# First x tile loaded in two column halves, and x, keys and values on one load queue in order of need: one change to the start of an attention kernel

## The chip, the cores and the metric

The kernel runs on one core of a Trainium2 chip. The metric is the device time of one execution in microseconds (us). A profile also gives a span, from the first to the last instruction; here the device time is about 1.8 us above it.

## The reference

`x` is 2048 x 512. It is normalised, goes through 32 heads of attention against cached keys and values (2048 x 128 per head), and through a two-layer network whose output gates the result.

```python
xn = layernorm(x)
q = (xn @ wq) per head                      # 32 heads of 128
p = softmax(q @ k.T * 128 ** -0.5)          # k, v: 32 x 2048 x 128
s = (p @ v) @ wo
g = silu(relu(xn @ w1 + b1) ** 2 @ w2 + b2)
out = x + s * g
```

## The kernel before

The program is a list of instructions for each engine, issued in order. What matters here is the start. The loads are issued from two queues, SP (SyncE) and AC (ScalarE):

```python
    ln_load(0, 0, SP)          # x tile 0, 128 rows
    ln_load(0, 1, AC)          # x tile 1
    load_k0(0)                 # keys of head 0, first half (SP)
    fill_wq(0, AC)             # query weights of head 0
    load_k0(1)                 # keys of head 0, second half (SP)
    E(AC, partial(_act, out=th_t[:, 0, 0:1], in_=warm[:, 0:1], func=ACT.Exp), deps=[t_warm])
    ln_load(0, 2, SP)
    ln_load(0, 3, SP)
    fill_wq(1)
    load_v0(0)
    load_v0(1)
    # ... further loads on SP
```

The work begins with 36 matmuls on zeros, which only keep TensorE busy. Then come the keys, transposed on TensorE, and the first x tile:

```python
    warm_up(36)
    k0_transpose(0)            # TensorE, 8 transposes, waits for the first half of the keys
    k0_copy(0)
    ln_bn(0, 0)                # VectorE, statistics of x tile 0
    ln_rstd(0, 0, eng=DV)
    ln_bn(0, 1)                # statistics of x tile 1
    ln_scale(0, 0)
    first_transpose(0)         # TensorE, 4 transposes of the scaled tile
    k0_transpose(1)            # TensorE, waits for the second half of the keys
    k0_copy(1)
    # ...
    first_copy(0)
    first_proj(0)              # TensorE, waits for the query weights
```

TensorE takes these in exactly this order, so the first half of the keys holds up everything behind it. About 1230 us of dense work follow.

The softmax here doesn't subtract the row's maximum and nothing guards it: scores larger than these inputs give would overflow.

## Time and profile before

| | before |
|---|---|
| device time, first three runs | 1237.87 us median (1237.75 to 1238.44) |
| span of the profiled run | 1236.3 us |
| TensorE busy | 1231.7 us (100%) |
| first half of the keys: issued, landed | 1.18, 5.20 us |
| last warm-up matmul ends | 5.00 us |
| first matmul on head 0's values | 9.68 us |

The prediction below shows the lines that carry this and reads them: the chain of the first 16 us, the timeline beside it, and the time of each load from issue to landing. The last row of the table is the start of the first eight matmuls named `psO<-v_sb,pT` in the timeline.

### The profile page before, as it was taken

What the parts mean: (1) busy time and instruction counts of PE and PEld (TensorE: products, weight loads), DVE (VectorE), ACT (ScalarE), POOL (GpSimd) and SP (SyncE); (2) the same over time, 40 slices, a digit from 0 to 9 for tenths busy, and PEclk for the clock granted to TensorE, in tenths of its full rate; (3) what the DMA queues carried; (4) which work ended last, traced back from release to release, by engine and by line L of the source; (5) the groups of instructions that cost most, each with busy time, mean ns of one, the idle gap of its engine ahead of it and who ended that gap; (6) DMA issues with size and microseconds to landing.
All of it is one profiled execution on the core that took longest, in us unless ns stands there. A gap on an engine that the chain in (4) does not pass through costs nothing.

```text
span 1236.3 us, 26934 instructions
## 1 busy us (share of the span) xinstructions
PE 1231.7 (100%) x11885; PEld 818.8 (66%) x11885; DVE 472.8 (38%) x953; ACT 1053.5 (85%) x1044; POOL 31.9 (3%) x73
## 2 busy tenths in 40 slices
PE   9999999999999999999999999999999999999999
PEld 7666666666666666666666666666666666666665
DVE  4453323244435332334444532333344333324333
ACT  7888888888888888888888888888888888888885
POOL 1010000000002000000000200000000000000000
PEclk9999999999999999999999999999999999999999
DMA  9999998777879897778778878787788789878771
GB/s 211 203 231 209 185 178 134 130 144 143 139 152 172 141 161 129 139 139 145 133 133 170 172 138 143 141 148 134 133 146 148 146 154 158 137 134 146 145 123 31
DMA packets 686868, 185.41 MB, mean 150 GB/s; under 512 B 673536, under 2 KB 685568, under 8 KB 686752
## 3 DMA queue, kind: packets, MB, share of 16 engines
q1 hardware_dynamic: 684656, 179.62, 80.4%
q0 software_dynamic: 1424, 3.81, 1.2%
q8 instruction: 94, 1.54, 0.6%
q10 hardware_dynamic: 672, 0.26, 0.1%
q14 instruction: 22, 0.18, 0.1%
HBM read 96.60 MB, written 2.10 MB: 80 GB/s over the span
## 4 chain that ended last, share of the span: by engine, by line
PE 99%; DMA 0%; DVE 0%; issue 0%; SPq 0%; DVEq 0%
PE psO L157 38%; PE psA L152 36%; PE psF L152 25%; DMA kT<-in_A_k_cache_dram 0%; PE psA L157 0%; DVE out_t L165 0%; PE psF L196 0%; DVE tmp_t L175 0%; PE psO L196 0%; PE psO L152 0%; DVE xnT L179 0%; SPq L208 0%; PE psA L196 0%; DVEq L119 0%
## 5 line engine op out<-in xcount | busy, mean ns | idle before, releaser
L161 ACT ACTIVATE pT<-psA 128x1024 bf16<-128x1024 f32 x1024 | 1043.5, 1023 | 163.5 <-PE psA L152 118.1
L157 PEld LDWEIGHTS psO<-v_sb,pT 128*128 128x128 bf16 x8192 | 547.7, 98 | 240.5 <-issue 12.5
L157 PE MATMUL psO<-v_sb,pT 128*128 128x129 bf16 x8192 | 631.6, 220 | 0.0
L152 PE MATMUL psA<-qt_sb,kT 128*128 128x512 bf16 x2032 | 604.8, 379 | 0.0
L179 DVE COPY o_un<-psO 128x258 f32<-128x258 f32 x256 | 97.4, 422 | 399.4 <-PE psO L157 398.7
L152 PE MATMUL psF<-xnT,wq_sb 128*128 128x512 bf16 (+1 forms) x520 | 168.9, 374 | 0.2 <-DVE xnT L179 0.2
L152 PE MATMUL psF<-wo_all,oT 128*128 128x512 bf16 x480 | 163.8, 379 | 0.0
L152 PEld LDWEIGHTS psA<-qt_sb,kT 128*128 128x128 bf16 x2032 | 156.9, 98 | 0.0
L179 DVE CAST qt_sb<-psF 128x512 bf16<-128x512 f32 (+1 forms) x130 | 88.0, 677 | 97.4 <-PE psF L152 97.4
L165 DVE TENSOR_TENSOR o_bf<-o_un,rden 128x512 bf16<-128x512 f32 x128 | 88.6, 692 | 4.7 <-DVE rden L183 0.3
L152 PEld LDWEIGHTS psF<-xnT,wq_sb 128*128 128x128 bf16 x520 | 50.2, 98 | 60.1 <-issue 0.3
L171 DVE TENSOR_SCALAR r_t<-psF,b1f 128x512 bf16<-128x512 f32 x56 | 42.0, 750 | 117.5 <-PE psF L152 117.5
L152 PEld LDWEIGHTS psF<-wo_all,oT 128*128 128x128 bf16 x480 | 46.9, 98 | 56.4
L152 PE MATMUL psF<-xnT,w_sb 128*128 128x512 bf16 x224 | 77.1, 379 | 0.0
L152 PE MATMUL psF<-w_sb,h2T 128*128 128x512 bf16 x224 | 74.2, 379 | 0.0
L152 PEld LDWEIGHTS psF<-xnT,w_sb 128*128 128x128 bf16 x224 | 21.9, 98 | 26.5
L152 PEld LDWEIGHTS psF<-w_sb,h2T 128*128 128x128 bf16 x224 | 21.9, 98 | 26.5
L165 DVE TENSOR_TENSOR z_t<-psF,b2bc 128x512 f32<-128x512 f32 x16 | 11.1, 692 | 67.2 <-PE psF L152 67.2
L165 DVE TENSOR_TENSOR acc<-psF,acc 128x512 f32<-128x512 f32 x28 | 19.3, 689 | 29.9 <-PE psF L152 29.9
L208 POOL DMA_DIRECT2D out_dram<-out_t x12 | 6.7, 554 | 891.0 <-DVE out_t L165 891.0
L165 DVE TENSOR_TENSOR h2T<-r_t 128x512 bf16<-128x512 bf16 x56 | 23.8, 425 | 1.9
L183 DVE RECIPROCAL rden<-o_un 128x4 f32<-128x4 f32 x128 | 22.9, 179 | 4.4
(47 smaller groups left out, 165.6 us busy)
## 6 DMA issues: line engine op xcount, KB each, us to landing
v_sb<-in_A_v_cache_dram SPq DMA_DIRECT2D x127, 512.0 KB, 4.7
wq_sb<-in_A_wq_dram SPq DMA_DIRECT2D x127, 128.0 KB, 3.1
wo_all<-in_A_wo_dram SPq DMA_DIRECT2D x4, 1024.0 KB, 6.7
w_sb<-in_B_w_dram SPq DMA_DIRECT2D x14, 256.0 KB, 4.3
oT<-o_bf SPq DMA_TRANSPOSE x128, 4.0
x_t<-in_A_x_dram POOLq DMA_DIRECT2D x16, 128.0 KB, 3.4
kT<-in_A_k_cache_dram SPq DMA_TRANSPOSE x127, 4.5
x_ln<-in_A_x_dram SPq DMA_DIRECT2D x15, 128.0 KB, 3.8
```

What stands on the lines that cost most here:

```text
L152: return e.matmul(out, lhsT, rhs, start=start, stop=stop)
L157: return e.matmul(out, lhsT, rhs, start=start, stop=stop, skip_group_check=True)
L161: return e.activation(out, in_, func, bias=bias, scale=scale)
L165: return e.tensor_tensor(out, in0, in1, op)
L171: return e.tensor_scalar(out, in0, scalar1=scalar1, scalar2=scalar2, op0=op0, op1=op1)
L179: return e.tensor_copy(out, in_)
L183: return e.reciprocal(out, in_)
L208: return e.dma_start(out, in_)
```

## The change

The intent: x tile 0 should be ready sooner, by reducing its left half while the right half still lands; and one queue, SP, should carry x, the keys and the values in the order in which they are needed, so that nothing less urgent is moved beside them. The first query weights stay on ScalarE's queue, where the first Exp, with its table load, now stands ahead of them.

```diff
-    ln_load(0, 0, SP)
-    ln_load(0, 1, AC)
+    HD = D // 2
+    sl_x0 = S.slot("x0b")
+    t_x0 = [S.emit_dma(SP, partial(_dma, out=x_ln[:, 0, c:c + HD], in_=A_x[0, 0:P, c:c + HD]), sl)
+            for c, sl in ((0, sl_xl[0]), (HD, sl_x0))]
+    ln_load(0, 1, SP)
     load_k0(0)
-    fill_wq(0, AC)
     load_k0(1)
     E(AC, partial(_act, out=th_t[:, 0, 0:1], in_=warm[:, 0:1], func=ACT.Exp), deps=[t_warm])
+    fill_wq(0, AC)
...
-    ln_bn(0, 0)
-    ln_rstd(0, 0, eng=DV)
+    for b in range(2):
+        t_xl[0] = t_x0[b]
+        ln_bn(0, 0, b * HD, (b + 1) * HD)
+    ln_rstd(0, 0, n=2, eng=DV)
     ln_bn(0, 1)
```

More of the change, by code (lines that the diff above doesn't have):

```diff
@@ L898, in bass_recurrent_scan__mha_block_cached__dense_activation_squared_relu__prompt_kernel @@
         at(j * SPB + SPB // 2, partial(load_xt, j))
-    HD = D // 2
     warm_up(36)
```

## The prediction

> **What bounds the kernel now.** I read the page first: busy shares, then the chain that ended last. Then I went to the first 16 us alone, because the diff only touches instructions emitted there.
>
> ```profile
> span 1236.3 us, 26934 instructions
> PE 1231.7 (100%) x11885; PEld 818.8 (66%) x11885; DVE 472.8 (38%) x953; ACT 1053.5 (85%) x1044; POOL 31.9 (3%) x73
> ...
> PE 99%; DMA 0%; DVE 0%; issue 0%; SPq 0%; DVEq 0%
> ```
>
> TensorE is busy 1231.7 of 1236.3 us and is 99% of the chain. It idles only 4.6 us: about 1 us before its first instruction, a few tenths around 5 to 8 us, and the rest in the output tail after 1231.5 us. So a change at the start can pay in one way only: TensorE's real work begins earlier or later and the whole 1230 us behind it shifts by that amount. The chain of the first 16 us says what that start hangs on (columns: start us, us, what):
>
> ```profile
> 0.73 0.40 SPq L208
> 1.12 0.06 issue
> 1.18 4.02 DMA kT<-in_A_k_cache_dram
> 5.20 0.05 issue
> 5.24 0.94 PE psO L196 x8
> 6.19 0.24 PE psF L196 x4
> 6.43 0.02 issue
> 6.45 0.43 DVE xnT L179
> 6.89 0.14 issue
> 7.02 0.38 PE psF L152 x4
> ```
>
> The gate is not the x tile but the first half of head 0's keys. SP issues it second, at 1.18; it lands at 5.20, and eight transposes of it come first in TensorE's order. Only after them come the four transposes of the normalised x tile, its copy, and the first projection, which needs the first query weights. The timeline of the same stretch shows what sits beside that chain:
>
> ```profile
> 0.72 0.40 ACTq L208 DMA_DIRECT2D x_ln<-in_A_x_dram  x1
> 0.73 0.40 SPq L208 DMA_DIRECT2D x_ln<-in_A_x_dram  x1
> ...
> 0.98 4.02 PE L152 MATMUL psA<-warm 128*128 128x128 bf16 x36 [0.98 <-POOL mhalf L187]
> ...
> 1.15 0.45 ACTq L208 DMA_DIRECT2D wq_sb<-in_A_wq_dram  x1
> 1.18 1.00 SPq L208 DMA_DIRECT2D kT<-in_A_k_cache_dram  x2
> ...
> 1.63 1.28 ACT L161 ACT_TABLE_LOAD   x1 [1.63 <-PEq L1025]
> ...
> 3.71 0.69 DVE L200 BATCH_NORM_STATS2 st_t<-x_ln 128x6 f32<-128x512 bf16 x1 [3.71 <-DMA x_ln<-in_A_x_dram]
> ...
> 5.50 0.41 DVE L171 TENSOR_SCALAR xn_t<-x_ln,mv_t,rstd 128x512 bf16<-128x512 bf16 x1
> ```
>
> Two things are to be seen. The warm-up matmuls fill TensorE from 0.98 to 5.00, so the key transposes could not start before 5.00 even if the keys were there: only 0.24 us of real waiting stands before 5.24. And the x path has slack: the scaled tile is ready at 5.91, while its transposes run only after the key transposes end, at 6.18. The DMA view cut down to these issues gives issue to landing (last column, us):
>
> ```profile
> kT<-in_A_k_cache_dram SPq DMA_DIRECT2D x1, 256.0 KB, 4.0
> x_ln<-in_A_x_dram ACTq DMA_DIRECT2D x1, 128.0 KB, 2.7
> x_ln<-in_A_x_dram SPq DMA_DIRECT2D x1, 128.0 KB, 3.0
> wq_sb<-in_A_wq_dram ACTq DMA_DIRECT2D x1, 128.0 KB, 4.2
> ```
>
> The first x tile lands at 3.7, the second at 3.4, the keys' first half at 5.2, the query weights at 1.15 + 4.2 = 5.35. In stretches of 0.2 us the DMA share is under 0.4 until 2.4 us and then stays near 1.0 at about 310 GB/s: from there the engines are shared, and what is queued beside a load decides when it lands.
>
> **What the Trainium skill says.** "DMA: Bandwidth & Descriptors", section "Issuing engines are not separate DMA queues": DMAs from different engines run on the same 16 DMA engines; issuing from two saves only issue time. The trace agrees: SP and ACT issue side by side at 0.73 and 0.72, 0.40 us each, then the share sits at 1.0. So moving x tile 1 to SP costs SP one issue and wins no bandwidth by itself. The same page, "Rules for kernel authors", says that transfers under 64 KB pay mostly overhead; the halves are exactly 64 KB. The trace shows the issue side of it: 0.40 us for 128 KB, 0.44 and 0.51 for 256 KB. "ScalarE: Activation LUTs", section "What ACT_TABLE_LOAD costs": about 1283 ns for the load; the trace has 1.28 us. This now stands ahead of the query weights' issue. "TensorE: Matmul & The Clock Gate", section "What you observe": matmuls 107 ns apart while the array is cold, about 4 us of them. Here 36 in 4.02 us is 112 ns each, which agrees and explains why the warm-up reaches to 5.00.
>
> **The change part by part.** (1) SP's order becomes x0 left, x0 right, x1, keys a, keys b. One issue to the next is 0.45 us (0.73 to 1.18), so the issues stand at 0.73, 1.18, 1.63, 2.08, 2.55, and everything behind moves by 2 x 0.45 = 0.9 us. (2) Statistics: one instruction of 0.69 becomes two of 0.42 (the trace has the 128x256 form in x tile 3), and the aggregate goes from 0.18 to 0.20. With the left half done while the right is landing, 0.42 + 0.20 replaces 0.69 + 0.18 behind the last landing: 0.25 us saved. For the right half I take 2.4 us to landing, less than x0's 3.0 because it has half the bytes and nothing beside it: 1.18 + 2.4 = 3.6, or 0.1 earlier. The reciprocal root is then there about 0.35 to 0.4 us sooner. x1 lands at about 1.63 + 2.6 = 4.2, before VectorE is ready for it at about 4.4, so the scaled tile comes near 5.6 instead of 5.91. All of this lies inside the slack and pays nothing by itself. (3) Keys a: issue 0.9 us later, but the query weights (131 KB, 0.42 us at 310 GB/s) no longer stand beside them. First heavy traffic came 1.5 us after its issue (0.73 to 2.3), so keys a should start near 3.55, move 262 KB at 310 GB/s in 0.85, and need about 0.5 for completion (x0 and x1, 262 KB, had been moved by about 3.05 and were reported at 3.4 to 3.7): 4.9, or 5.1 with some traffic of the weights beside it. Against 5.20 that is 0.1 to 0.3 sooner, and the warm-up allows at most 0.24. (4) Query weights: ACT now does table load (from about 0.95, when the warm tile is set), Exp 0.21, then the issue at about 2.4. With the same 4.2 to landing they come at 6.6; the projection reads them at 7.02, at the earliest 6.8 after the shift. Slack 0.2 to 0.4. The sum: TensorE's useful work starts 0.1 us earlier in the middle case, which moves the end by 0.1 us.
>
> **The rivals.** A: the warm-up is the new bound. Keys land before 5.00, the wait of 0.24 goes, the end is 1237.6. It is the best case, and speaking for it is the saturated share, which says bytes and not issue times set 5.20. B: the keys keep their 4.0 us behind a later issue: 2.08 + 4.0 = 6.1, TensorE starts 0.85 late, 1238.7. Speaking for it: other 256 KB loads in this stretch take 4.0 to 5.4. Against: those had more bytes ahead of them. C: the query weights take the place of the keys. With the 5.1 us that a later 128 KB weight load took, they land at 7.5, 0.5 late at the first projection: 1238.4. Against: some slack, and their old 4.2 was under just as much traffic. D: the shift of 0.9 starves something later. Values a, issued at 3.64 and 5.0 to landing, go from 8.6 to 9.5 against a first use at 9.68; head 1's transposed keys go from 11.3 to 12.2 against 16.8; head 1's values from 15.4 to 16.3 against 17.7. All hold, the first just so.
>
> **Range and chances.** I give A and the middle case together 0.6, B or C in some degree 0.35, D 0.05. The weighted shift is -0.15 x 0.6 + 0.5 x 0.4 = +0.1 us, so about none. I take the middle case of a slight gain, 1237.8 us. The runs of before spread over 0.7 us, so the range is 1236.8 to 1239.1: half a spread and more beyond the best case, and B with some spread above. For 2% it takes 25 us; nothing in the first 8 us can make that, since TensorE works without a gap from then on: faster 0.004, same 0.99, slower 0.006.
>
> **What would show each step.** Right: statistics on 256 columns starting before 3.7; the right half landed near 3.6; keys a landing at 4.8 to 5.2 in spite of an issue at about 2.1; the key transposes starting at 5.0 to 5.2; the weights' issue on ACT at about 2.4; first scores at 7.7 to 7.9 instead of 7.96; TensorE's busy time unchanged within 0.3 us. Wrong: key transposes starting at 5.5 or later (B), or the first projection waiting for a DMA of the query weights rather than for the copied x tile (C), or a wait of TensorE for values between 9 and 18 us (D). A change over 2 us would mean that work far from the start moved, which I see no way for.

## The result, and the profile after

The changed kernel took 1238.47 us median (1238.12 to 1239.61, six runs), the kernel before 1237.94 us (1237.75 to 1238.45, six runs). The ratio is 1.0006, with an interval of 0.9993 to 1.0018: the same within 2%, and not told apart from zero by that interval.

The six spans of the changed kernel are more telling: 1237.8, 1237.8, 1236.3, 1236.5, 1236.8, 1236.5. Two executions stand 1.0 us or more above the others. The profile is of one of those two. This is its chain in the first microseconds (start us, us, what):

```profile
0.72 0.40 SPq L208
...
1.18 0.42 SPq L208
...
1.64 0.42 SPq L208
...
2.11 3.65 DMA kT<-in_A_k_cache_dram
...
5.80 1.04 PE psO L196 x8
6.84 0.43 PE psF L196 x4
```

The chain has the same members as before, but the keys' first half is issued at 2.11 instead of 1.18 and lands at 5.76 instead of 5.20. Three issues of x stand ahead of it instead of one. The timeline shows what was beside it:

```profile
0.72 1.28 ACT L161 ACT_TABLE_LOAD   x1 [0.72 <-PEq L1029]
...
0.96 0.42 ACTq L208 DMA_DIRECT2D wq_sb<-in_A_wq_dram  x1
...
3.72 0.43 DVE L200 BATCH_NORM_STATS2 st_t<-x_ln 128x6 f32<-128x256 bf16 x1 [0.63 <-DMA x_ln<-in_A_x_dram]
...
5.80 1.04 PE L196 MATMUL psO<-ident,kT 128*128 128x128 bf16 x8 [0.80 <-DMA kT<-in_A_k_cache_dram]
```

TensorE stood idle for 0.80 us before the keys, where it had been 0.24. The weights' load was issued at 0.96 while the table load was still running, so it did not wait for the table at all. These are the landings (last column, us from issue) of the right x half, the keys and the weights:

```profile
x_ln<-in_A_x_dram SPq DMA_DIRECT2D x1, 64.0 KB, 2.5
...
kT<-in_A_k_cache_dram SPq DMA_DIRECT2D x1, 256.0 KB, 3.6
...
wq_sb<-in_A_wq_dram ACTq DMA_DIRECT2D x1, 128.0 KB, 2.5
```

The right half of x tile 0 lands at 1.18 + 2.5 = 3.7, no sooner than the whole tile did before. The weights land near 3.5, two microseconds earlier than before and well ahead of their use.

The second thing to see is the rate of the matmuls. These are the groups by form between 5 and 10 us, first of the kernel before, then of the changed kernel (count, busy us, mean ns of one, idle before them):

```profile
L196 PE MATMUL psO<-ident,kT 128*128 128x128 bf16 x16 | 1.6, 257 | 0.2 <-DMA kT<-in_A_k_cache_dram 0.2
...
L196 PE MATMUL psF<-ident,xn_t 128*128 128x128 bf16 x8 | 0.8, 221 | 0.0
```

```profile
L196 PE MATMUL psO<-ident,kT 128*128 128x128 bf16 x16 | 2.1, 312 | 0.8 <-DMA kT<-in_A_k_cache_dram 0.8
L196 PE MATMUL psF<-ident,xn_t 128*128 128x128 bf16 x8 | 1.2, 311 | 0.0
```

One transpose took 312 ns here against 220 ns where TensorE runs at its full rate; the 257 of before is a mix of slow ones (mean 295 in the first eight) and fast ones (220 in the second). In the changed kernel's profile everything stays slow until about 10.1 us. The first matmul on values starts at 11.23 instead of 9.68, 1.55 us later, and the span is 1.5 us longer. So the whole difference arises before 11.3 us.

### The profile page after: what moved, and what is told of

Same layout as the page of the kernel before. It is cut to its first block, busy times and chain, and to the rows that moved or that the text cites. A ratio compares the mean times of both kernels' runs of the same rounds, so it can differ in the third digit from the quotient of the medians.

```text
span 1237.8 us, 26729 instructions
## 1 busy us (share of the span) xinstructions
PE 1222.1 (99%) x11678; PEld 820.7 (66%) x11885; DVE 472.8 (38%) x954; ACT 1054.6 (85%) x1044; POOL 32.0 (3%) x73
## 4 chain that ended last, share of the span: by engine, by line
PE 98%; issue 1%; DMA 0%; DVE 0%; SPq 0%; DVEq 0%
PE psO L157 38%; PE psA L152 35%; PE psF L152 25%; PE psA L157 0%; DMA kT<-in_A_k_cache_dram 0%; PE psO L196 0%; PE psF L196 0%; DVE out_t L165 0%; SPq L208 0%; DVE tmp_t L175 0%; PE psO L152 0%; DVE xnT L179 0%; PE psA L196 0%; DVEq L119 0%
## 5 line engine op out<-in xcount | busy, mean ns | idle before, releaser
L152 PE MATMUL psA<-qt_sb,kT 128*128 128x512 bf16 x1840 | 562.9, 379 | 10.1
L152 PE MATMUL psF<-xnT,wq_sb 128*128 128x512 bf16 (+1 forms) x508 | 165.9, 375 | 0.3
```

The lines of the kernel that those rows point to most:

```text
L152: return e.matmul(out, lhsT, rhs, start=start, stop=stop)
```

## The experiments

Two theories stand against each other after this. **C (clock ramp)**: what makes a run slow is the idle stretch after the warm-up. It can fall into the stretch of time by which TensorE's rate is decided, and then the slow matmuls last some microseconds longer. **L (lateness only)**: the keys come late and everything moves with them; the two runs of 1237.8 were chance. Twelve kernels ran. The first four shared one chip and nine runs of the kernel before, all the others a second chip and nine or ten of its runs.

**The changed kernel again.** No edit.

> The changed kernel once more, for the spread of its runs. Theory C (clock ramp): the keys land at about 5.76, the gap in TensorE of 0.8 us after the warm-up falls in some executions into the stretch that decides when matmuls go from 312 to 220 ns, so the spans come in two groups, near 1236.4 (most) and near 1237.8 (some), with a mean 0.3 to 0.8 us above the kernel before. Rival L (lateness only): the keys come 0.56 us late and everything moves by that, so the spans lie in one group near 1236.9, and the two runs of 1237.8 do not come back.

Measured: 1238.14 us median against 1237.97, ratio 1.0002 (0.9989 to 1.0014). Spans 1236.1 to 1236.8, no slow one in five. The keys landed at 2.11 + 3.45 = 5.56, TensorE idled 0.63 us, and yet the span of the profiled run was 1236.3, as in the kernel before. The groups between 5 and 10 us show why:

```profile
L196 PE MATMUL psO<-ident,kT 128*128 128x128 bf16 x16 | 1.2, 220 | 0.7 <-DMA kT<-in_A_k_cache_dram 0.6
...
L196 PE MATMUL psF<-ident,xn_t 128*128 128x128 bf16 x8 | 0.8, 220 | 0.0
```

All sixteen transposes of the keys are fast here. The first eight took 0.62 us on the chain, against 0.94 in the profile of before. The lateness of 0.37 us was almost wholly won back. This run alone decides nothing between C and L; it shows that the same program's transposes of the keys execute at either rate.

**No idle stretch.** The warm-up lengthened to the keys' landing.

```diff
 (changed kernel)
-    warm_up(36)
+    warm_up(43)
```

> The changed kernel with 43 instead of 36 warm-up matmuls, so that they end at about 5.78 and leave no gap before the keys. No load moves. Theory C: no span above 1237.3, median within 0.5 us of the kernel before, and in the profile the matmuls reach 220 ns by 7.5. Rival L: spans as in the changed kernel, since the keys land no earlier, with runs of 1237.8 as often as there.

Measured: 1238.38 us median, ratio 1.0003 (0.9989 to 1.0017); spans 1236.2 to 1236.8. The chain now reads:

```profile
0.98 4.77 PE psA L152 x43
5.75 0.76 PE psO L196 x8
```

The wait for the keys is gone from it, and the full rate came by 6.5 us. No execution was slow. That agrees with C, but it is weak evidence: with 3 slow ones in 16 runs of the changed kernel (all its runs), five runs without one happen often enough by chance.

**The idle stretch alone, in the kernel before.** No load is touched; only the warm-up ends earlier.

```diff
 (kernel before)
-    warm_up(36)
+    warm_up(29)
```

> The kernel before with 29 instead of 36 warm-up matmuls: they end at about 4.2, so a gap of about 1.0 us opens before the keys at 5.2. No load moves. Theory C: the gap alone makes runs 1 to 1.5 us longer appear (spans near 1237.3 to 1237.8) in a third or more of the executions. Rival L: keys land at 5.2 as before, so every span stays within 0.2 of 1236.3.

Measured: spans 1237.2, 1237.4, 1236.0, 1236.0, 1237.1; ratio 1.0005 (0.9992 to 1.0017). Three of five executions are 1.1 to 1.4 us longer than the other two, with nothing between. The keys landed at 5.03 in the profile, not late at all. The profiled run is one of the slow ones; this is its group of key transposes from 4.9 to 10 us:

```profile
L196 PE MATMUL psO<-ident,kT 128*128 128x128 bf16 x16 | 2.1, 312 | 0.8 <-DMA kT<-in_A_k_cache_dram 0.8
```

This is the line of the changed kernel's slow run, idle stretch and all, without the change. L has no place for it. The run also shows that in the other executions the same idle stretch costs nothing: 1236.0 is as good as the kernel before gets.

**A longer idle stretch.**

```diff
 (kernel before)
-    warm_up(36)
+    warm_up(22)
```

> The kernel before with 22 instead of 36 warm-up matmuls: they end at about 3.45 and leave a gap of some 1.7 us before the keys at 5.2. Theory C (clock ramp, the gap must not fall into the deciding stretch): with so little work ahead of the gap no execution gets the fast matmuls before it, so the two groups of the run with 29 become one, all slow: every span at 1236.9 or above, mean near 1237.3, and the profile shows matmuls of 312 ns until at least 8.3. Rival L: spans of 1236.0 to 1236.5 as in the kernel before, because the keys land at the same time.

Measured: spans 1237.7, 1237.6, 1236.7, 1237.2, 1236.8, mean device time 1.08 us above the kernel before of the same chip; ratio 1.0008 (0.9994 to 1.0021). In the profile, with 1.50 us idle, matmuls stay at 312 ns until about 11 us. The two groups are gone and all runs are longer than any of the nine runs of the kernel before beside them (at most 1236.5). My bound of 1236.9 was missed by two runs. L is refuted by both shortened warm-ups.

**The weights off ACT's queue.** A test of the failed step of the prediction.

```diff
 (changed kernel)
-    fill_wq(0, AC)
+    fill_wq(0, SP)        # behind both halves of the keys
```

> The changed kernel with the first query weights taken from ACT's queue and put on SP behind the keys. Tests the step of the prediction that failed: if the weights' 131 KB beside the keys cost their bytes, the keys land 0.3 to 0.4 us earlier than 5.76, at 5.35 to 5.5; if 3.65 us is what this transfer takes for its own sake, they land at 5.7 again. The weights would be issued at about 3.06 and land at 6.5 to 7.2; if later than the copied x tile at 7.0 the first projection waits for them. Time within 0.7 us of the changed kernel either way.

Measured: 1238.33 us median, ratio 1.0003 (0.999 to 1.0015). The keys landed at 2.12 + 3.28 = 5.40. That is what I had written down for the bytes theory, but the changed kernel's own profiles have 5.76, 5.56, 5.28 (with the long warm-up) and 5.60, so 5.40 lies among them and the test is inconclusive. One reason is in the changed kernel's own landings: the weights were in by 3.5 us, so they had moved ahead of the keys, not beside them. The first projection started at 6.94 and waited for x, not for the weights.

**The halving undone.**

```diff
 (changed kernel)
-    t_x0 = [S.emit_dma(SP, ... two column halves ...)]
+    ln_load(0, 0, SP)
...
-    for b in range(2): ... ln_bn(0, 0, b * HD, (b + 1) * HD)
-    ln_rstd(0, 0, n=2, eng=DV)
+    ln_bn(0, 0)
+    ln_rstd(0, 0, eng=DV)
```

> The changed kernel with the first x tile loaded whole again (one issue, one statistics instruction), all else as changed. The keys are then issued at 1.65 instead of 2.11. If the late keys come from the two extra issues ahead of them, they land 0.45 earlier than in the changed kernel, at 4.9 to 5.3, the gap after the warm-up is at most 0.3, and every span lies in the band of the kernel before, 1236.0 to 1236.9. If the move of the weights behind Exp is what matters, the keys land at 5.6 or later and the gap stays.

Measured: the keys' first half landed at 5.27, as expected, but the kernel got slower, not faster: 1238.96 us median, spans 1236.4 to 1238.0, ratio 1.0009 (0.9996 to 1.0022). The expectation of no run over 1236.9 failed. A new wait had appeared: the second half of the keys landed at 7.39, where it had been about 6.0 before. The two longest of the five runs (1237.9 and 1238.0) have a mean granted clock of 0.999; the other three, and all runs of the changed kernel, have 1.000. The section on all profiles shows what a mean of 0.999 stands for; these two runs were not profiled. I ran the kernel again, beside the changed one.

> The changed kernel with x tile 0 whole, again, for one open point: its first run lost 0.66 us waiting for the second half of the keys (7.39), where the loads moved only 94 to 153 GB/s from 4.0 to 4.8 us. If that dip belongs to this order of loads, the second half lands after 6.9 again and the mean is again 0.5 us or more above the changed kernel of the same rounds. If it was chance, the second half lands near 6.2, and the mean is at or below that of the changed kernel.

> The changed kernel a third time, to stand on the same chip as the next one. Theory C: spans in the two groups seen so far, most at 1236.0 to 1236.8, none to two of five at 1237.1 to 1237.9; keys land at 5.3 to 5.8.

Measured, on the same chip: the changed kernel 1238.36 us median, spans 1236.4, 1236.8, 1236.6, 1236.3, 1237.8, ratio 1.0006 (0.9992 to 1.002); with the whole tile 1238.72, spans 1236.7 to 1237.2, ratio 1.0007 (0.9993 to 1.002). The changed kernel had one slow run of five again. The late second half came back too (timeline and stretches of the repeated run; in the stretches the columns are the window, its length, TensorE busy, granted clock, DMA share, GB/s):

```profile
7.18 0.62 PE L196 MATMUL psO<-ident,kT 128*128 128x128 bf16 x8 [0.58 <-DMA kT<-in_A_k_cache_dram]
```

```profile
4.00:4.40 0.40, 0.40 (x7) 1.00 0.59 160
4.40:4.80 0.40, 0.40 (x6) 1.00 0.68 149
```

From 4.0 to 4.8 us the loads moved about 150 GB/s at a share near 0.6, where the kernel before had about 300 at a share above 1.0. So the dip belongs to this order of loads and not to chance; the mean was only 0.18 us above the changed kernel's, less than I had written. What causes the dip stays open: no view told which engines lagged. With the halving it did not come: in the five profiles that have it with x on one queue, the second half landed at 6.1 to 6.4.

**The halving alone.** The two halves put into the kernel before, with x tile 1 and the weights left on ACT.

> The kernel before with only the halving: x tile 0 in two loads and two statistics, x tile 1 and the weights on ACT as before. The keys are issued at 1.65 instead of 1.18. If bytes ahead of them and not their issue set the landing, they land at 5.1 to 5.3 as before and nothing changes (spans 1235.9 to 1236.6). If each issue ahead costs its time, they land at 5.6, the gap is 0.6, and one or two spans of five come at 1237.0 or more.

Measured: 1238.31 us median, spans 1236.1 to 1236.7, ratio 1.0003 (0.9989 to 1.0017). The keys were issued at 1.67 and landed here:

```profile
1.67 3.64 DMA kT<-in_A_k_cache_dram
```

That is 5.31. The kernel before and its two versions with a shorter warm-up, whose loads are the same, had 5.20, 5.03 and 4.97. So an issue 0.49 us later cost between 0.1 and 0.35 us of landing, by this one profile: part of it, not all. The halves landed together here (both statistics ran back to back from 3.58), so nothing of their idea was gained.

**Keys on the other queue.** An attempt to have the keys in before the warm-up ends.

```diff
 (kernel before)
     ln_load(0, 0, SP)
-    ln_load(0, 1, AC)
-    load_k0(0)
-    fill_wq(0, AC)
-    load_k0(1)
+    load_k0(0, AC)
+    fill_wq(0, SP)
+    load_k0(1, AC)
+    ln_load(0, 1, SP)
```

> The kernel before with its queues exchanged: both halves of the keys on ACT's queue from 0.72, x tiles 0 and 1 and the weights on SP. The keys land at 4.2 to 4.6, before the warm-up ends at 5.00, so the key transposes start at 5.0 (0.24 earlier than before) and TensorE has no gap there. Theory C and L both say a gain of about 0.2 us, spans 1235.8 to 1236.5; more only if the matmuls are fast from 5.0 on. If the weights on SP land late, the first projection waits and the gain is lost.

> The same with 30 warm-up matmuls, which end at 4.33. If keys really land at 4.2 to 4.6, the key transposes start at 4.4 to 4.7, and the next limit is VectorE: statistics of x tile 1 stand ahead of the scaling of tile 0, so its transposes start near 5.6 and TensorE idles about 0.3 to 0.5. L: first scores at 7.4 to 7.6, a gain of 0.3 to 0.5. C: the same in most executions, with some of them slow by up to 1 us where the idle stretch falls badly.

Both failed. With 36 warm-up matmuls: 1240.53 us median, ratio 1.0021 (1.0008 to 1.0033); with 30: 1241.1, ratio 1.0026 (1.0013 to 1.0038). The keys landed at 4.9 and 5.1 instead of 4.2 to 4.6, and x tile 0, alone at the head of its queue, took 4.3 and 4.1 us instead of 3.0: it came at 5.1 and 4.8. The longer wait was for x tile 1, now behind the weights: it landed at 6.54 and 6.61, and its statistics stand ahead of the scaling of tile 0 in VectorE's order. So the scaled tile was late, and TensorE idled 2.10 and 1.56 us for it. The stretches of the first one hold something more (window, length, busy us and count of TensorE, its weight loads, VectorE, ScalarE and GpSimd, then granted clock, DMA share, GB/s):

```profile
4.50:5.50 1.00, 0.81 (x13) 0.50 (x9) 0.41 (x1) 0.00 (x0) 0.00 (x0) 1.00 1.13 349
5.50:7.60 2.10, 0.03 (x1) 0.00 (x0) 1.65 (x6) 1.02 (x1) 0.57 (x1) 1.00 1.29 271
...
8.60:9.60 1.00, 1.00 (x11) 0.78 (x9) 0.46 (x3) 0.50 (x1) 0.00 (x0) 0.50 1.29 162
```

After an idle stretch of 2.1 us the granted clock is 0.50, and the eight transposes that follow, from 8.00, take 1.06 us, the slow rate. Before the idle stretch they had been fast (0.62 for eight). This is the one profile in which a view names the slow rate as half clock; in all others the views show 1.00 over the slow matmuls at the start. The next section says why.

**A candidate to beat both.** Only the weights moved, to SP behind the keys; x tile 1 stays on ACT.

```diff
 (kernel before)
     load_k0(0)
-    fill_wq(0, AC)
     load_k0(1)
+    fill_wq(0, SP)
```

> Candidate to beat both: the kernel before with only the first weights moved, from ACT's queue to SP behind the keys. Keys are issued at 1.18 as before with 131 KB fewer beside them. If the bytes theory of the prediction holds, they land at 4.8 to 5.0, the wait of 0.24 after the warm-up goes, and the spans lie at 1235.7 to 1236.3, about 0.2 below the kernel before. If a single queue moves fewer bytes in the same time, as the changed kernel suggests, they land at 5.1 to 5.3 and nothing is gained.

Measured: 1237.94 us median against 1237.92, ratio 1.0001 (0.9988 to 1.0013), six runs within 1236.1 to 1236.4. The keys landed at 4.43, 0.5 to 0.8 us sooner than in the three profiles with the loads of the kernel before, and sooner than I had expected. In the timeline TensorE takes them without a wait (the full rate came during the warm-up in this profile, so it ended at 4.77), and then:

```profile
4.61 0.61 PE L196 MATMUL psO<-ident,kT 128*128 128x128 bf16 x8
5.68 0.40 PE L196 MATMUL psF<-ident,xn_t 128*128 128x128 bf16 x4 [0.47 <-DVE xn_t L171]
6.22 0.62 PE L196 MATMUL psO<-ident,kT 128*128 128x128 bf16 x8
```

What the keys gained turned into waits for the scaled x tile (0.47 us) and for the second half of the keys, which landed at 6.17. The first matmul on values started at 9.48 instead of 9.68, but the mean time did not fall. It beats the changed kernel by 0.6 us in the mean of their rounds and equals the kernel before.

**All profiles together.** The start of the first matmul on values, taken from each timeline, the span, and the time from which the trace holds a record of a granted clock of 1.00:

| kernel | first value matmul, us | span, us | difference | full clock recorded from, us |
|---|---|---|---|---|
| before | 9.68 | 1236.3 | 1226.6 | 5.96 |
| changed (slow run) | 11.23 | 1237.8 | 1226.6 | 10.12 |
| changed again | 9.72 | 1236.3 | 1226.6 | 4.82 |
| changed, third | 9.78 | 1236.4 | 1226.6 | 5.74 |
| changed, 43 warm-ups | 10.01 | 1236.6 | 1226.6 | 6.29 |
| changed, weights on SP | 9.60 | 1236.2 | 1226.6 | 5.57 |
| changed, tile whole | 10.56, 10.30 | 1237.2, 1236.9 | 1226.6, 1226.6 | 6.70, 6.21 |
| before, 29 warm-ups | 10.61 | 1237.2 | 1226.6 | 9.82 |
| before, 22 warm-ups | 11.12 | 1237.7 | 1226.6 | 10.97 |
| before, halves | 9.82 | 1236.4 | 1226.6 | 6.12 |
| before, weights on SP | 9.48 | 1236.2 | 1226.7 | 4.39 |
| keys on ACT, 36 and 30 | 12.17, 13.02 | 1238.7, 1239.6 | 1226.5, 1226.6 | 4.29 (then 0.50 from 7.70 to 11.12), no record |

Whatever the start does, the rest takes 1226.5 to 1226.7 us. All that this change can do is done in the first 10 us or so.

The last column comes from the clock records in the packed traces (runs/<label>/trace.npz), which no view lists; a view shows 1.00 over any time that has no record. Matmuls before the first record are slow, those after it fast, and the three profiles of slow runs have it at 9.8 to 11.0 us, all others that hold one at 4.3 to 6.7. In the run with keys on ACT, the changes at 4.29, 7.70 and 11.12 are 3.41 us apart.

Counting back in steps of 3.41 us from each first record gives a test of theory C. In the last step before it, TensorE was idle (by its recorded matmuls) for at most 0.64 us in every profile that holds such a record. In the three slow runs the step before that one, ending at 6.4 to 7.6 us, held 0.80, 0.82 and 0.87 us of idle time, and the full rate did not come. So in these profiles a step with 0.8 us or more of idle time brings no full rate, one with 0.64 us or less does, and a miss costs another 3.41 us at the slow rate. The steps lie differently against the program in each execution, so the same kernel comes out both ways. The fall at 7.70 ended a step with 2.3 us of idle time. Over 1237 us, one step at 0.50 makes a mean of 0.9986: that is the 0.999 of this run, and so, by estimate, of the two longest runs with the tile whole.

## Why the prediction was right or wrong, point by point

**Right: where the end is set.** The prediction said that any effect is a shift of TensorE's start and arrives at the end one for one. The table shows it over a range of 3.5 us. It also said that work far from the start would not move, and that 2% was out of reach. The measured median lies within its range, which was wide enough to hold rival B, and the change made no difference clear of noise.

**Wrong in sign: the central case.** The prediction had a gain of 0.1 us. Over all its runs here (16) the changed kernel averaged 1238.51 us, the kernel before (25 runs) 1238.01: 0.50 us slower, on two chips for the later runs. Three of the 16 were the slow ones with spans of 1237.8, of which one was profiled; without them the mean is 1238.26, 0.25 us slower. So about half of the loss is the rare slow start. The other half fits the lateness of the keys, but no run separates it from noise.

**The step that failed: part 3, the keys at 4.9 to 5.1.** They landed at 5.76, 5.56 and 5.60, so it was rival B (a late landing), at about half its size. The working was start at 3.55, 0.85 to move, 0.5 to complete. Adding up the bytes of the changed kernel's 0.1 us stretches, an amount of 655 KB, that of x, weights and keys, had been moved by about 4.5 us in its three profiles, close to the 4.4 of the working. The mis-sized term is what comes after: 1.1 to 1.25 us from there to the landing, not 0.5. The trace shows of what it is made. It holds sixteen reports for each load, and the load has landed with the last. Thirteen of the sixteen for the keys were in by 4.93, 5.02 and 4.96 us in the three profiles of the changed kernel, as predicted; the last came at 5.76, 5.56 and 5.60. From the first report to the last it took 1.24 to 1.27 us, and 0.85 us in the kernel before. The 0.5 was taken from the x tiles, which had stood at the head of their queues: there, in the kernel before, the sixteen reports lie within 0.36 and 0.40 us. So the prediction priced a load that arrives together, and the keys arrived with a few late parts. Why those parts were late, no run shows.

**Wrong: the weights no longer stand in the way (parts 3 and 4).** They were expected at ACT's queue at 2.4, behind a table load from 0.95 and Exp. The table load started at 0.72, and the weights were issued at 0.96, during it. No run shows why; the instruction that issues a load evidently did not wait for ScalarE's own work. So the order meant for them was not what the chip did, their bytes still went ahead of the keys, and rival C of the prediction (a late weights load) never came near.

**Where the bytes argument held.** Taking the weights away from beside the keys did bring them in sooner where they really stood there: in the kernel before, from 4.97 to 5.20 down to 4.43, more than the 0.42 us of their bytes. It paid nothing because the next waits were near: the scaled x tile and the second half of the keys.

**Right, with one exception: statistics and slack (part 2).** The halves took 0.43 us each, the aggregate 0.21. The scaled tile was begun at 5.28 instead of 5.50, and it paid nothing, being inside the slack. The right half landed at 3.7, not 3.6. In the repeated run x tile 1 came at 4.92 instead of 4.2, and the scaling began only at 5.55, still without cost.

**Missed: the rate of the matmuls.** The prediction read the 112 ns of the warm-up matmuls as the cold rate, but took the warm-up only as a bound in time. It had no rival in which an idle stretch of some 0.8 us costs not itself but the rate of what follows. The two kernels with shortened warm-ups show that such a stretch alone, with no load moved, makes executions 0.5 to 1.6 us longer. The Trainium skill, "TensorE: Matmul & The Clock Gate", section "What's actually happening", says that the array is throttled by default, is released after about 3.4 us of sustained work, and that the window in which this is judged runs freely and is not tied to the kernel's start. The trace agrees: the changes of the granted clock lie 3.41 us apart, the full clock comes between 4.29 and 10.97 us, and in the three slow profiles it comes one step late, after a step with 0.80 to 0.87 us of idle time.

**Rival D** did not come: no profile has a wait of TensorE for values.

## What to carry to other kernels

When one engine is busy to the end, read the head of the program only as far as that engine's first real instruction, and find the one load that stands first in its order: adding issues ahead of that load can cost something even when bytes seem to set the pace (here up to 0.35 us for one issue), and removing others beside it soon meets the next wait. A filler that keeps TensorE busy should reach to the landing of the first data, since an idle stretch of 0.8 us behind it kept the slow rate for another 3.4 us in some executions here. Where single runs of one kernel stand a full microsecond apart, look at the mean duration of one matmul in each profile, and at the time of the first clock record, before comparing medians.

## What the Trainium skill lacked or had wrong

- "TensorE: Matmul & The Clock Gate", section "HAM oscillation — how this bites in real kernels", gives the rule that idle gaps above about 3.4 us are to be avoided. Here 2.1 us of idle time at full rate was followed by a granted clock of 0.50 (one profile, keys on ACT's queue), and idle stretches of 0.8 and 1.5 us before the full rate was reached kept matmuls at 312 ns until about 10 and 11 us. How much idle time a window may hold and still release the clock, I found on no page: in these profiles 0.64 us did not prevent it and 0.80 us did.
- No page that I read says that a profile's clock records begin only with the first change, so that a view fills the slow start with 1.00: the slow run's first record is at 10.12 us, and the keys' transposes ahead of it took 312 ns each under a shown 1.00. The mean duration of one matmul, or the record itself, shows the state.
- "ScalarE: Activation LUTs", section "What ACT_TABLE_LOAD costs", gives the duration (1.28 us here, as stated), but not that ScalarE's queue goes on past it: a load placed behind the table load and an Exp was issued at 0.96 us, with the table load running from 0.72 to 2.00 and the Exp starting at 2.02.
- "DMA: Bandwidth & Descriptors", section "Rules for kernel authors", advises against splitting a transfer into partition halves and says nothing of column halves. Here the column halves cost one issue of about 0.46 us; in the kernel before, the load behind them landed 0.1 to 0.35 us later (one profile).
- The same page says that the engines take turns between the queues, but not how long a load at the head of its queue then waits, nor that a load's sixteen parts can land far apart (1.24 to 1.27 us for the keys in the changed kernel). With keys and x tile on separate queues, a 128 KB tile at the head of its queue took 4.1 to 4.3 us to land, against 2.7 to 3.0 where the other queue began with as small a load.
